# Block 0 of a fused attention, dense and expert kernel: its steps issued in another order

## The chip, the cores and the metric

The kernel runs on one core of one Trainium2 chip, as one launch. The metric is the device time in microseconds; lower is better. Five engines work side by side, each through its own instructions in program order, and wait for each other by semaphores: TensorE (PE in the rows: matrix products and transposes, results into PSUM), VectorE (DVE), ScalarE (ACT), GpSimd (POOL) and SyncE (SP, which issues most transfers).

## What is computed

Three layers follow each other on 3072 tokens (4 sequences of 768) of width 384:

```
for t in range(S):                      # per batch b and head h, D = 48
    cur = np.einsum('bhd,bhe->bhde', u[None] * kt, vt)
    y[:, :, t] = np.einsum('bhd,bhde->bhe', rt, state + cur)
    state = wt[:, :, :, None] * state + np.einsum('bhd,bhe->bhde', kt, vt)
x = y as (3072, 384)
h = x @ w_in                            # 384 -> 2048
x = (maximum(h, 0) + alpha * minimum(h, 0)) @ w_out
expert_idx = argmax of (x / |x|) @ (expert_emb / |expert_emb|).T / tau
out = gate * (maximum(x @ w1[e], 0) @ w2[e])     # the chosen one of 8 experts per token
```

## The kernel before, in words

The tokens are cut into 24 tiles of 128, and three tiles make a block: eight blocks. A tile first goes through chunked attention, then its block through the dense layer (2048 hidden features in 16 groups f of 128), then all tokens through the experts. The dense part is a software pipeline over a step counter T: step T = 16 j + f issues the first layer's product for group f of block j (`l1`, nine matmuls into `h_ps`, L409), and the second layer's for the group two steps back (`l2`, nine matmuls into `o_ps`, L433). Each value is carried as a high and a low part in a reduced float format, so that three products replace one. After `l1`, ScalarE scales `h_ps` by alpha into `m` (L413), VectorE takes the minimum of both (`m`, L414), ScalarE rounds it to the high part `gh` (L417), and VectorE subtracts for the low part `gl` (L423, function `l1_lo`).

During block 0 (T = 0 to 15, and a written-out list PLAN ahead of it, which includes `l1` of f = 0 and 1) three other kinds of work stand between these products:

- **Weight passes** `conv(q, ...)`: the weights come as 64-bit words in 16 staged groups c (even: w_in, odd: w_out; each serves two f). Pass 0 is ScalarE (L196), pass 1 two VectorE operations (L198, L199), pass 2 the high part on ScalarE (L210), pass 3 the low part on VectorE (L212). At step T, pass 0 handles c = T+4, pass 1 c = T+3, pass 2 c = T+3 and pass 3 c = T+2. When pass 3 of a group is issued, SyncE is told to load group c+4 into a free staging buffer (there are four).
- **Logit work** `wprime_a` and `wprime_b`: extra columns of w_out that give the router's logits directly. For each w_out group, `wprime_a` transposes the weights on TensorE (`wt_ps`, L232, two PSUM buffers) and ScalarE copies them out to `wt` (L234, L235); one step later `wprime_b` multiplies by the normalized expert rows `enT` (`wq_ps`, L243), and ScalarE copies (L247, L248).
- **Attention pieces** `ATT[q](n)` of the three tiles of block 1 (n = 3, 4, 5, whose pieces start at T = 0, 4, 8). Pieces 0 and 1 are the decay scans with what follows from them on VectorE (L261 to L267; L270, after which ScalarE reads the weights, L278). 6 and 7 prepare r and the diagonal (L288; `dg_ps`, L300; L304; L309). 2 and 3 transpose k (`kt_ps`, L323; `Kt`, L324) and make the scores (`a_ps`, L333; ScalarE `A`, L336; a GpSimd mask). 4 gives `y_ps` and the new state `u_ps` (L346 to L369). 5 transposes y into the next block's `xh`, `xl` (L383 to L385). For tile n they run at T = t0, t0+1, t0+2, t0+4, t0+6 and t0+7.

All small PSUM results (`kt_ps`, `a_ps`, `dg_ps`, `u_ps`, `y_ps`, `t_ps`, `wt_ps`, `wq_ps`, `ep`) take turns in one pool of three buffers, `ps_a`; `h_ps` has two buffers of its own. A product that takes its turn waits until the one three turns back has been read.

In PLAN, `aq.n` is attention piece q of tile n, `cq.c` a weight pass, `l1.f` a first-layer product, `p0.g` and `p1.g` the logit work, and `wN` N matmuls whose result nobody reads. `s` normalizes the eight expert rows and transposes them into `enT`. No scheduler intervenes: each engine's order is the order of issue.

Of the kernel before, what the change touches and what calls it, by code (L numbers as in the profile page):

```python
# [8 lines left out]
F32 = mybir.dt.float32  # L9
# [4 lines left out]
AF = mybir.ActivationFunctionType  # L14
# [12 lines left out]
KD = DM // 128  # L27
NE = 8
# [36 lines left out]
WPD = (2, 3)  # L65
# [4 lines left out]
OFF = 4  # L70
# [4 lines left out]
LAGS = [0, 1, 4, 4, 6, 7, 2]  # L75

LOADS = [(0, "w"), (0, "rk"), "id", "v", (0, "n"), "e", (1, "w"), (1, "rk"), (1, "n"), (2, "w"), (2, "rk"), (2, "n"), 0, 1, 2, 3, "u"]
PLAN = "a0.0 a1.0 a8.0 a2.0 w6 a6.0 a3.0 a7.0 w8 a0.1 a1.1 a6.1 a4.0 a3.1 a9.0 a2.1 c0.0 a7.1 a9.1 w8 a0.2 c0.1 c0.2 a1.2 a6.2 c1.0 a4.1 w8 a3.2 c1.1 a7.2 a5.0 a5.1 c2.0 w4 a4.2 p0.0 c3.0 a5.2 c2.1 c1.2 l1.0 c3.1 c2.2 l1.1 c0.3 c3.2 s p1.0 a8.1 a2.2 a9.2"

AT1 = [0, 4, 8]  # L80
AT = {2: [-1, 6], 3: [-4, 1, 7]}
# [12 lines left out]
def tile_main(ctx, tc, keep, x2d, tbl, att, w_in, w_out, alpha, u_row, u_col, emb, tau, w1, w2, cst, out):  # L94
    nc = tc.nc
    PE, DVE, ACT, POOL, SP = nc.tensor, nc.vector, nc.scalar, nc.gpsimd, nc.sync
# [12 lines left out]
    ps_a = ctx.enter_context(tc.tile_pool(name="ps_a", bufs=3, space=bass.MemoryType.PSUM))  # L109

    identr, idsx, wix, cnt = keep
    ident = identr.bitcast(F32)
# [6 lines left out]
    enT = cp.tile([128, KD, NE], F32, name="enT")  # L119
# [26 lines left out]
    en = att2[0:NE, LD:LD + DM]  # L146
# [10 lines left out]
    def load_att(n, part=None):  # L157
        if n not in ld_t:
            if n == 2:
                ld_t[n] = att2[:, 0:LD]  # L160
            else:
                ld_t[n] = ldp.tile([128, LD], F32, tag="ld", name="ld")
        m = LN + 2 * DM if n in ND else LN
        for s in {None: [slice(0, LN), slice(m, LD)] if n in ND else [slice(0, LD)], "w": [slice(LD - LW, LD)], "rk": [slice(0, LN)], "n": [slice(m, LD - LW)]}[part]:
            SP.dma_start(out=ld_t[n][:, s], in_=att[n][:, s])
# [10 lines left out]
    NG = 8  # L176
# [4 lines left out]
    def load_stage(kind, g):  # L181
        t = sgp.tile([128, GF * DM, 2], I32, tag="sg", name="stg")
        if kind == "in":
            for k in range(KD):
                SP.dma_start(out=t[:, k * GF * 128:(k + 1) * GF * 128, :], in_=w_in[:, k, 2 * g * GF * 128:2 * (g + 1) * GF * 128])
        else:
            SP.dma_start(out=t, in_=w_out[:, g * GF:(g + 1) * GF, :])
        stage[kind, g] = t

    def conv(q, kind, g):  # L190

        t = stage[kind, g]
        lw, hw = t[:, :, 0], t[:, :, 1]
        lf = lw.bitcast(F32)
        if q == 0:
            ACT.activation(out=lf, in_=lw.bitcast(U32), func=AF.Copy, scale=-0.936 * 2.0 ** -51, bias=-2.0)  # L196
        elif q == 1:
            DVE.scalar_tensor_tensor(out=lw, in0=hw, scalar=3, in1=lw, op0=ALU.logical_shift_left, op1=ALU.bitwise_or)  # L198
            DVE.scalar_tensor_tensor(out=lw, in0=hw, scalar=0x3FFFFFFF, in1=lw, op0=ALU.bitwise_or, op1=ALU.bitwise_and)  # L199
        else:  # L200
            h, g0 = divmod(g, NG // 2)
            if kind == "in":
                hi, lo = (w[:, :, g0 * GW:(g0 + 1) * GW] for w in win[h])
            else:
                if h == len(wout):
                    wout_half()
                hi, lo = (w[:, g0 * GF:(g0 + 1) * GF, 0:DM] for w in wout[h])
            f3 = lf.rearrange("p (a b) -> p a b", a=(KD if kind == "in" else GF))
            if q == 2:
                ACT.activation(out=hi, in_=f3, func=AF.Copy, scale=-1.0)  # L210
            else:
                DVE.scalar_tensor_tensor(out=lo, in0=f3, scalar=-1.0, in1=hi.bitcast(F32), op0=ALU.mult, op1=ALU.subtract)  # L212
                del stage[kind, g]
# [175 lines left out]
    def warm(n):  # L389

        for _ in range(n):
            t = ps_h.tile([128, 3, 128], F32, tag="h", name="idle")
            PE.matmul(out=t, lhsT=oneb, rhs=oneb.rearrange("p (o t) -> p o t", o=1).to_broadcast([128, 3, 128]), start=True, stop=True)
# [4 lines left out]
    g_t, m_t, o_t = {}, {}, {}  # L398
# [22 lines left out]
    def l1_lo(j, f):  # L421
        gh, gl = g_t[j, f]
        DVE.tensor_tensor(out=gl, in0=m_t.pop((j, f)), in1=gh.bitcast(F32), op=ALU.subtract)  # L423
# [376 lines left out]
    if True:  # L800
# [40 lines left out]
        for n in range(B0[NB - 1], NTILE):  # L841
            c, b = divmod(n, B)
# [5 lines left out]
        for n in range(NTILE):  # L848
            j = max(q for q in range(NB) if B0[q] <= n)
# [7 lines left out]
        def run(kind, *a):  # L857
            if (kind, *a) in ran:
                return
            if kind != "w":  # L860
                ran.add((kind, *a))
            if kind == "a":
                q, n = a
                ATT[q](n)
                m = n + 3 if n < 2 else n + 2
                if q in (4, 8, 9) and n != 2 and m < NTILE and (n > 2 or {("a", i, n) for i in (4, 8, 9)} <= ran):
                    load_att(m)
            elif kind == "c":
                q, c = a
                conv(q, ("in", "out")[c % 2], c // 2)  # L870
                if q == 3 and c + NSG < 2 * NG:
                    load_stage(("in", "out")[(c + NSG) % 2], (c + NSG) // 2)
            elif kind == "w":
                warm(*a)
            elif kind == "l":
                (l1, l2)[a[0] - 1](0, a[1])
            elif kind == "p":
                (wprime_a, wprime_b)[a[0]](a[1])
            else:
                DVE.tensor_scalar(out=en2, in0=en2, scalar1=1e-6, scalar2=None, op0=ALU.add)  # L880
                DVE.reciprocal(out=en2, in_=en2)
                ACT.activation(out=en, in_=en, func=AF.Copy, scale=en2)
                ep = ps_a.tile([128, KD, NE], F32, tag="a", name="ep")
                for k in range(KD):
                    PE.transpose(ep[:, k, :], en[:, k * 128:(k + 1) * 128], ident[0:NE, 0:NE])
                ACT.activation(out=enT, in_=ep, func=AF.Copy)

        def pieces(T, qs):
            for q, n in sched.get(T, []):
                if q in qs:  # L890
                    run("a", q, n)
                    if q == 6:
                        run("a", 7, n)

        def convs(T, late):
            for q, i in CONV[late]:
                c = T + OFF - i
                if 0 <= c < 2 * NG:
                    run("c", q, c)
# [43 lines left out]

        for t in PLAN.split():
            run(t[0], *(int(i) for i in t[1:].split(".") if i))
        for T in range(16 * NB + 2):
            j, f = divmod(T, 16)
            for i, d in enumerate(WPD):
                c = T + OFF - d
                if c % 2 and 0 <= c < 2 * NG:  # L950
                    run("p", i, c // 2)
            convs(T, 0)
            pieces(T, (2, 3, 4, 5))
            if 0 <= T and j < NB:
                run('l', 1, f) if j == 0 else l1(j, f)
            if T == 16 * (NB - 1):
                xg.extend(atp.tile([128, 2, ROW], F32, tag=t, name="xg") for t in ("st", "st", "at"))
                for t in xg:
                    POOL.memset(t, 0.0)
            if T >= 2:  # L960
                run('l', 2, T - 2) if T < 18 else l2((T - 2) // 16, (T - 2) % 16)
                if (T - 2) % 16 == 15:
                    o_evac((T - 2) // 16)
                    q = (T - 2) // 16
                    bg.append(chain(route(q), *((early_table(), early_loads()) if q == NB - 2 else (last_table(),) if q == NB - 1 else ())))
            if T >= 0:
                pieces(T, (0, 1, 6, 8))
                convs(T, 2)
                if (j, f) in m_t:
                    l1_lo(j, f)  # L970
                convs(T, 1)
            step(STEP7 if j >= NB - 1 else 1)
            if T == 32:
                zero = sgp.tile([128, DM], F32, tag="sg", name="zero")
                POOL.memset(zero, 0.0)
            if 32 <= T < 32 + NTILE:
                SP.dma_start(out=out[(T - 32) * CH:(T - 31) * CH, :], in_=zero)
            for fn, i, at in EARLY:
                if T - 16 * NB == at:
                    (split, x_T)[fn](0, i)  # L980
# [350 lines left out]
```

## Time and profile before

| | us |
|---|---|
| median of 3 runs (lowest, highest) | 824.95 (823.55, 826.72) |
| the profiled execution's own time | 825.29 |
| its span, first to last instruction | 823.5 |
| TensorE busy, weight loads busy | 791.7, 753.9 |
| VectorE, ScalarE, GpSimd busy | 584.3, 436.4, 297.3 |
| mean granted TensorE clock | 0.989 of full |

The profiled execution lies 0.34 us above the median of the runs. Granted clock 1.00 is 2.4 GHz and 0.50 is 1.2 GHz. The span begins with some 34 us of first loads and attention of block 0, then come block 0's dense steps up to about 123 us, then seven blocks, and the experts. A busy share here is an average over all of them; only the stretch from about 12 to 123 us is touched by the change.

### The profile page before, as it was taken

To read this page: it belongs to the slowest core of one execution; us is meant where nothing else is said; L and a number is where in the kernel's file an instruction comes from. 1 tells how busy PE (TensorE), PEld (TensorE's weight loads), DVE (VectorE), ACT (ScalarE), POOL (GpSimd) and SP (SyncE) were. 2 spreads that over 40 slices of the span, in tenths; PEclk is the share of its full clock that TensorE was granted. 3 is DMA by queue.
4 is the path that set the end of the run, shared out by engine and by line. 5 is a ranking of instruction groups with operands and counts; after the bars stand their busy time and mean duration, and the time that the engine had idled before them with its cause. 6 is when DMAs were issued, how large, how long until landed. Compare 5 with 4: busy or idle time off the path is not lost. (4 is left out here: it accounts for less than half of the span.)

```text
span 823.5 us, 16482 instructions
## 1 busy us (share of the span) xinstructions
PE 791.7 (96%) x6462; PEld 753.9 (92%) x6462; DVE 584.3 (71%) x1229; ACT 436.4 (53%) x861; POOL 297.3 (36%) x365
## 2 busy tenths in 40 slices
PE   8788999999999999999999999998899999999996
PEld 5588899998999999999999999896899999999996
DVE  7879857886686586686676674637987677768662
ACT  5676645444345435444444443326556776767662
POOL 2101112233224124124224212154466776767731
PEclk9979999999999999999999999999999999999998
DMA  9555410235324313113113101054756787687740
GB/s 325 186 163 168 180 69 2 75 118 135 121 84 146 127 33 102 69 58 98 69 69 97 68 2 30 30 215 150 189 204 208 274 289 241 223 275 224 265 165 33
DMA packets 31623, 114.86 MB, mean 139 GB/s; under 512 B 5756, under 2 KB 13148, under 8 KB 29232
## 3 DMA queue, kind: packets, MB, share of 16 engines
q0 software_dynamic: 13952, 59.86, 22.1%
q1 hardware_dynamic: 17584, 53.85, 19.6%
q8 instruction: 53, 0.87, 0.5%
q14 instruction: 34, 0.28, 0.2%
HBM read 99.36 MB, written 15.51 MB: 139 GB/s over the span
## 5 line engine op out<-in xcount | busy, mean ns | idle before, releaser
L413 ACT ACTIVATE m<-h_ps,al_sb 128x384 f32<-128x384 f32 x128 | 74.1, 579 | 125.2 <-PE h_ps L409 120.3
L414 DVE TENSOR_TENSOR m<-h_ps,m 128x384 f32<-128x384 f32 x128 | 71.0, 554 | 97.8 <-ACT m L413 97.0
L417 ACT ACTIVATE gh<-m 128x384 fp32r<-128x384 f32 x128 | 67.2, 525 | 122.6 <-DVE m L414 122.0
L423 DVE TENSOR_TENSOR gl<-m,gh 128x384 fp32r<-128x384 f32 x128 | 80.6, 630 | 35.0 <-ACT gh L417 34.3
L337 POOL TENSOR_SCALAR_AFFINE_SELECT A<-A 128x512 f32<-128x512 f32 x48 | 30.3, 654 | 186.8 <-ACT A L336 186.8
L686 POOL DMA_INDIRECT raw<-in_w,wix x64 | 67.4, 1053 | 51.3 <-DVE w0l L698 23.2
L728 PE MATMUL h_ps<-yh,w0h 128*128 128x256 f32 x264 | 77.1, 292 | 3.4 <-DVE g2l L733 2.7
L728 PE MATMUL h_ps<-yl,w0h 128*128 128x256 f32 x264 | 74.7, 283 | 0.9 <-DVE yl L719 0.9
L728 PE MATMUL h_ps<-yh,w0l 128*128 128x256 f32 x264 | 74.3, 281 | 0.0
L698 DVE TENSOR_TENSOR w1l<-raw,w1h 128x768 fp32r<-128x768 f32 x64 | 60.7, 954 | 18.5 <-ACT w1h L697 14.5
L409 PE MATMUL h_ps<-xh,win0h 128*128 128x384 f32 x192 | 69.3, 361 | 2.3 <-DVE m L414 1.5
L698 DVE TENSOR_TENSOR w0l<-raw,w0h 128x768 fp32r<-128x768 f32 x64 | 60.7, 958 | 12.2 <-ACT w0h L697 11.3
L409 PE MATMUL h_ps<-xh,win1h 128*128 128x384 f32 x192 | 68.3, 356 | 0.2 <-DVE m L414 0.2
L433 PE MATMUL o_ps<-wout1h,gh 128*128 128x392 f32 x192 | 65.3, 340 | 0.5 <-issue 0.4
L433 PE MATMUL o_ps<-wout0l,gh 128*128 128x392 f32 x192 | 65.7, 342 | 0.0
L433 PE MATMUL o_ps<-wout1h,gl 128*128 128x392 f32 x192 | 65.4, 341 | 0.2 <-issue 0.2
L433 PE MATMUL o_ps<-wout0h,gh 128*128 128x392 f32 x192 | 65.7, 342 | 0.0
L409 PE MATMUL h_ps<-xl,win0h 128*128 128x384 f32 x192 | 65.5, 341 | 0.2 <-DVE xl L385 0.2
L433 PE MATMUL o_ps<-wout0h,gl 128*128 128x392 f32 x192 | 65.5, 341 | 0.0
L433 PE MATMUL o_ps<-wout1l,gh 128*128 128x392 f32 x192 | 65.4, 340 | 0.0
L409 PE MATMUL h_ps<-xh,win0l 128*128 128x384 f32 x192 | 65.3, 340 | 0.0
L409 PE MATMUL h_ps<-xh,win1l 128*128 128x384 f32 x192 | 64.9, 338 | 0.0
(282 smaller groups left out, 2258.5 us busy)
## 6 DMA issues: line engine op xcount, KB each, us to landing
ld<-in_att SPq DMA_DIRECT2D x18, 1348.5 KB, 5.6
stg<-in_w_in SPq DMA_DIRECT2D x24, 256.0 KB, 4.9
stg<-in_w_out SPq DMA_DIRECT2D x8, 768.0 KB, 4.0
x2d<-rows SPq DMA_DIRECT2D x24, 194.0 KB, 6.9
out<-zero SPq DMA_DIRECT2D x24, 192.0 KB, 6.9
ld<-in_att SPq DMA_DIRECT2D x5, 512.0 KB, 3.8
ld<-in_att SPq DMA_DIRECT2D x3, 452.5 KB, 5.2
raw<-in_w,wix POOLq DMA_INDIRECT x64
```

Of the source, the lines that this page charges most:

```text
L337: POOL.affine_select(out=h, in_=h, pattern=[[0, HP], [1, CH]], compare_op=ALU.is_gt, fill=0.0, base=0, channel_multiplier=-1)
L409: PE.matmul(out=h, lhsT=w[:, k, :], rhs=x[:, k, :], start=(n == 0), stop=(n == 3 * KD - 1))
L413: ACT.activation(out=m, in_=h, func=AF.Copy, scale=al_sb[:, f:f + 1])
L414: DVE.tensor_tensor(out=m, in0=h, in1=m, op=ALU.min)
L417: ACT.activation(out=gh, in_=m, func=AF.Copy)
L423: DVE.tensor_tensor(out=gl, in0=m_t.pop((j, f)), in1=gh.bitcast(F32), op=ALU.subtract)
L433: PE.matmul(out=o_t[j][i], lhsT=g[:, s], rhs=w, start=(f == 0 and n == 0), stop=(f == KF - 1 and n == 2))
L686: POOL.indirect_dma_start(out=t, out_offset=None, in_=src, in_offset=idx(wix[:, h, COL[s]:COL[s] + 1]))
L698: DVE.tensor_tensor(out=lo, in0=a, in1=hi.bitcast(F32), op=ALU.subtract)
L728: PE.matmul(out=h, lhsT=w[:, k, :], rhs=x[:, k, :], start=(n == 0), stop=(n == 3 * KD - 1))
```

## The change

Only the order of issue in PLAN and in block 0's steps is changed.

```
-PLAN = "... a6.1 a4.0 a3.1 a9.0 a2.1 c0.0 ... c3.0 a5.2 c2.1 c1.2 l1.0 c3.1 c2.2 l1.1 c0.3 c3.2 s p1.0 a8.1 a2.2 a9.2"
+PLAN = "... a6.1 s a4.0 a3.1 a9.0 a2.1 e c0.0 ... c3.0 a5.2 c2.1 c1.2 l1.0 c3.1 c2.2 l1.1 p1.0 c0.3 c3.2 w4 a8.1 a2.2 a9.2"
...
+            elif kind == "e":
+                ep = ps_a.tile([128, KD, NE], F32, tag="a", name="ep")
+                for k in range(KD):
+                    PE.transpose(ep[:, k, :], en[:, k * 128:(k + 1) * 128], ident[0:NE, 0:NE])
+                ACT.activation(out=enT, in_=ep, func=AF.Copy)
             else:
                 DVE.tensor_scalar(out=en2, in0=en2, scalar1=1e-6, scalar2=None, op0=ALU.add)
                 DVE.reciprocal(out=en2, in_=en2)
                 ACT.activation(out=en, in_=en, func=AF.Copy, scale=en2)
-                ep = ps_a.tile([128, KD, NE], F32, tag="a", name="ep")
-                for k in range(KD):
-                    PE.transpose(ep[:, k, :], en[:, k * 128:(k + 1) * 128], ident[0:NE, 0:NE])
-                ACT.activation(out=enT, in_=ep, func=AF.Copy)
...
             j, f = divmod(T, 16)
-            for i, d in enumerate(WPD):
-                c = T + OFF - d
-                if c % 2 and 0 <= c < 2 * NG:
-                    run("p", i, c // 2)
+            pieces(T, (2, 3, 4, 5))
             convs(T, 0)
-            pieces(T, (2, 3, 4, 5))
             if 0 <= T and j < NB:
                 run('l', 1, f) if j == 0 else l1(j, f)
...
-            if T >= 0:
-                pieces(T, (0, 1, 6, 8))
-                convs(T, 2)
-                if (j, f) in m_t:
-                    l1_lo(j, f)
-                convs(T, 1)
+            for i, d in enumerate(WPD):
+                c = T + OFF - d
+                if c % 2 and 0 <= c < 2 * NG:
+                    run("p", i, c // 2)
+            convs(T, 2)
+            if j == 0 and (j, f) in m_t:
+                l1_lo(j, f)
+            pieces(T, (0, 1, 6, 8))
+            if j and (j, f) in m_t:
+                l1_lo(j, f)
+            convs(T, 1)
```

So the expert rows (`s`, and their transposes, now `e`) go into the first loads' time; in PLAN the first `wprime_b` directly follows `l1` of f = 1, and four idle matmuls (`w4`) stand ahead of tile 2's k transposes; in each step attention pieces 2 to 5 come ahead of weight passes 0 and 1, the logit work comes behind both layers' products, and pieces 0, 1, 6 and 8 come behind weight pass 3 and `l1_lo`.

On ScalarE, at steps 3 and 4, before the change (`gh` of step 3 is the second row; `A` holds tile 3's scores):

```order
L413 ACTIVATE m<-h_ps,al_sb 128x384
L417 ACTIVATE gh<-m 128x384
L210 ACTIVATE win0h<-stg 128x3x256
L247 ACTIVATE s_wp<-wq_ps 128x16
L248 ACTIVATE wout0h<-s_wp 128x2x8
L196 ACTIVATE stg<-stg 128x768
L324 ACTIVATE Kt<-kt_ps 128x512
L336 ACTIVATE A<-a_ps 128x512 x2
L413 ACTIVATE m<-h_ps,al_sb 128x384
```

And in the changed kernel:

```order
L413 ACTIVATE m<-h_ps,al_sb 128x384
L417 ACTIVATE gh<-m 128x384
L234 ACTIVATE wt<-wt_ps_815 128x512
L235 ACTIVATE wt<-wt_ps_816 128x256
L210 ACTIVATE win0h<-stg 128x3x256
L324 ACTIVATE Kt<-kt_ps 128x512
L336 ACTIVATE A<-a_ps 128x512 x2
L196 ACTIVATE stg<-stg 128x768
L413 ACTIVATE m<-h_ps,al_sb 128x384
```

The two copies out of `wt_ps` now stand directly behind `gh` of step 3, where the copy of `wq_ps` stood behind a weight pass; and the weight pass L196 has moved behind the scores. The same holds at steps 7 and 8, and 11 and 12.

On VectorE, at step 1 (the second scan of tile 3, L270), before:

```order
L198 SCALAR_TENSOR_TENSOR stg<-stg 128x768
L199 SCALAR_TENSOR_TENSOR stg<-stg 128x768
L270 SCALAR_TENSOR_TENSOR PS<-ld,anew 128x519
L212 SCALAR_TENSOR_TENSOR wout0l<-stg,wout0h 128x2x384
L423 TENSOR_TENSOR gl<-m,gh 128x384
L198 SCALAR_TENSOR_TENSOR stg<-stg 128x768
L199 SCALAR_TENSOR_TENSOR stg<-stg 128x768
L414 TENSOR_TENSOR m<-h_ps,m 128x384
```

And in the changed kernel:

```order
L198 SCALAR_TENSOR_TENSOR stg<-stg 128x768
L199 SCALAR_TENSOR_TENSOR stg<-stg 128x768
L212 SCALAR_TENSOR_TENSOR wout0l<-stg,wout0h 128x2x384
L423 TENSOR_TENSOR gl<-m,gh 128x384
L270 SCALAR_TENSOR_TENSOR PS<-ld,anew 128x519
L198 SCALAR_TENSOR_TENSOR stg<-stg 128x768
L199 SCALAR_TENSOR_TENSOR stg<-stg 128x768
L414 TENSOR_TENSOR m<-h_ps,m 128x384
```

The scan has moved two operations back. The same holds at step 5 for tile 4 and at step 9 for tile 5. The order of SyncE's transfers is the same in both kernels.

## Rows read from the trace of the kernel before

**Rows 1.** Busy time by stretch: us, then PE, PEld, DVE, ACT, POOL, granted clock, DMA.

```profile
34.00:51.00 17.00, 10.46 (x142) 9.41 (x142) 13.55 (x21) 13.01 (x28) 0.89 (x2) 0.60 0.59 188
...
60.00:83.00 23.00, 20.71 (x260) 19.24 (x259) 20.54 (x31) 16.14 (x34) 3.71 (x6) 1.00 0.54 179
...
106.00:123.00 17.00, 17.00 (x198) 16.51 (x196) 8.06 (x14) 7.83 (x16) 3.42 (x5) 1.00 0.24 84
```

**Rows 2.** Timeline of TensorE: start, duration, instruction, idle before it and releaser.

```profile
37.96 0.48 PE L885 MATMUL ep<-ident,att 8*128 8x8 f32 x3 [3.94 <-ACT att L882]
...
45.29 0.89 PE L243 MATMUL wq_ps<-enT,wt 128*32 128x8 f32 x48 [1.63 <-ACT wt L234]
...
46.59 0.52 PE L409 MATMUL h_ps<-xl,win0h 128*128 128x384 f32 x1
...
48.84 0.52 PE L409 MATMUL h_ps<-xh,win0l 128*128 128x384 f32 x1
...
56.35 0.59 PE L243 MATMUL wq_ps<-enT,wt 128*32 128x8 f32 x48
...
58.39 1.16 PE L333 MATMUL a_ps<-ld 64*128 64x128 f32 x14 [0.45 <-ACT s_wp L247]
59.47 0.44 PE L409 MATMUL h_ps<-xh,win0h 128*128 128x384 f32 x1
```

**Rows 3.** Timeline of VectorE.

```profile
15.37 0.56 DVE L369 TENSOR_TENSOR y<-y_ps,dv 128x384 f32<-128x384 f32 x1 [1.78 <-PE y_ps L367]
...
37.43 0.96 DVE L198 SCALAR_TENSOR_TENSOR stg<-stg 128x768 int32<-128x768 int32 x1 [0.27 <-ACT stg L196]
...
43.85 0.96 DVE L198 SCALAR_TENSOR_TENSOR stg<-stg 128x768 int32<-128x768 int32 x1 [1.12 <-ACT stg L196]
...
45.72 1.23 DVE L270 TENSOR_TENSOR_SCAN PS<-ld,anew 128x519 f32<-128x519 f32 x1
...
50.98 0.56 DVE L414 TENSOR_TENSOR m<-h_ps,m 128x384 f32<-128x384 f32 x1 [0.83 <-ACT m L413]
...
52.69 0.56 DVE L309 TENSOR_TENSOR dv<-ld,dg 128x384 f32<-128x384 f32 x1 [0.55 <-ACT dg L304]
...
56.36 0.55 DVE L414 TENSOR_TENSOR m<-h_ps,m 128x384 f32<-128x384 f32 x1
...
68.98 1.23 DVE L270 TENSOR_TENSOR_SCAN PS<-ld,anew 128x519 f32<-128x519 f32 x1
70.13 0.93 DVE L212 SCALAR_TENSOR_TENSOR wout0l<-stg,wout0h 128x768 fp32r<-128x768 f32 x1
...
71.45 0.95 DVE L198 SCALAR_TENSOR_TENSOR stg<-stg 128x768 int32<-128x768 int32 x1
```

**Rows 4.** Timeline of ScalarE.

```profile
39.62 0.18 ACT L247 ACTIVATE s_wp<-wq_ps 128x16 f32<-128x16 f32 x1 [0.95 <-PE wq_ps L243]
...
46.98 0.72 ACT L278 ACTIVATE ld<-ld,wmid 128x512 f32<-128x512 f32 x1 [0.68 <-DVE PS L270]
...
50.39 0.56 ACT L413 ACTIVATE m<-h_ps,al_sb 128x384 f32<-128x384 f32 x1
...
53.38 0.59 ACT L234 ACTIVATE wt<-wt_ps 128x512 f32<-128x512 f32 x1
...
56.95 0.52 ACT L417 ACTIVATE gh<-m 128x384 fp32r<-128x384 f32 x1 [1.44 <-DVE m L414]
...
70.25 0.72 ACT L278 ACTIVATE ld<-ld,wmid 128x512 f32<-128x512 f32 x1 [0.62 <-DMA stg<-in_w_in]
...
73.55 0.58 ACT L413 ACTIVATE m<-h_ps,al_sb 128x384 f32<-128x384 f32 x1
```

**Rows 5.** TensorE alone by stretch: us, busy, granted clock, DMA share, GB/s.

```profile
37.00:38.00 1.00, 0.04 (x1) 0.55 1.02 426
...
51.00:52.00 1.00, 1.00 (x10) 1.00 0.43 178
...
569.00:571.00 2.00, 0.15 (x2) 1.00 1.00 381
```

More of the change, by code (lines that the diff above doesn't have):

```diff
@@ L77 @@
 LOADS = [(0, "w"), (0, "rk"), "id", "v", (0, "n"), "e", (1, "w"), (1, "rk"), (1, "n"), (2, "w"), (2, "rk"), (2, "n"), 0, 1, 2, 3, "u"]
-PLAN = "a0.0 a1.0 a8.0 a2.0 w6 a6.0 a3.0 a7.0 w8 a0.1 a1.1 a6.1 a4.0 a3.1 a9.0 a2.1 c0.0 a7.1 a9.1 w8 a0.2 c0.1 c0.2 a1.2 a6.2 c1.0 a4.1 w8 a3.2 c1.1 a7.2 a5.0 a5.1 c2.0 w4 a4.2 p0.0 c3.0 a5.2 c2.1 c1.2 l1.0 c3.1 c2.2 l1.1 c0.3 c3.2 s p1.0 a8.1 a2.2 a9.2"
+PLAN = "a0.0 a1.0 a8.0 a2.0 w6 a6.0 a3.0 a7.0 w8 a0.1 a1.1 a6.1 s a4.0 a3.1 a9.0 a2.1 e c0.0 a7.1 a9.1 w8 a0.2 c0.1 c0.2 a1.2 a6.2 c1.0 a4.1 w8 a3.2 c1.1 a7.2 a5.0 a5.1 c2.0 w4 a4.2 p0.0 c3.0 a5.2 c2.1 c1.2 l1.0 c3.1 c2.2 l1.1 p1.0 c0.3 c3.2 w4 a8.1 a2.2 a9.2"
 AT1 = [0, 4, 8]
```

## The prediction, made before the changed kernel ran

> **What bounds the kernel now.** First the busy times by stretch, since the change touches only the time up to 123 us. From 34 to 51 us, where TensorE's longest waits lie, TensorE is busy 10.46 of 17.00 us at a mean clock of 0.60, while VectorE is busy 13.55 and ScalarE 13.01 [rows 1]. From 60 to 83, a stretch with one attention tile in it, VectorE (20.54 of 23.00) and TensorE (20.71) are close to each other; from 106 to 123 TensorE works all 17.00 us and VectorE less than half of them [rows 1].
>
> Then the timelines, for who waits last. TensorE stands 3.94 us before the expert rows' transposes `ep` and 1.63 us before the second `wq_ps` [rows 2]. Its clock falls while it stands: 0.55 in the slice from 37 to 38, and full again in the slice from 51, after it had worked without a gap since 45.29 [rows 2, 5]. That looks like some 5.6 us of waiting to be had, and more at the low clock. But what does the next step wait for? `m` of step 2 on VectorE starts at 50.98 and waited 0.83 us for ScalarE's `m` at 50.39, not for a product [rows 3, 4]. ScalarE is behind because it stood 0.68 us for the scan L270, up to 46.98 [rows 4]. And L270 started at 45.72 because VectorE had been working since 37.43, with a single wait, the 1.12 us before 43.85 [rows 3]. So in this stretch the path goes through the weight passes and the scan on VectorE and ScalarE; TensorE waits beside them. That is what the reader is to see: the largest idle time of the busiest engine is here not on the path.
>
> **The change, step by step.** Times are those of the profiled execution (825.29 us), which is 0.34 above the median of the runs; the sum is carried over to the median.
>
> (a) Expert rows early. Their two tiny VectorE operations fall into the 1.78 us for which VectorE waits before 15.37 [rows 3], and ScalarE waits for the same products. Without that cover they would cost under 1 us. The transposes `ep` are new in TensorE's row there and take one of the three `ps_a` turns, so that `dg_ps` of tile 1 waits for a copy. `ep` took 0.48 us at its old place, at a low clock [rows 2]. Between nothing and 0.48 I take +0.3, which TensorE hands on to the first `l1`.
>
> (b) The first `wprime_b` no longer waits, but its copies now stand ahead of weight pass 0 of group 3 on ScalarE. L247 takes 0.18 [rows 4]; with L248, about as long, I estimate 0.35. VectorE's row of passes therefore starts 0.65 later, at 38.08 in place of 37.43 [rows 3]. Its 1.12 us wait goes, because tile 2's `Kt` and state come sooner. L270 is now behind L212 and `gl`, which take 71.45 - 70.13 = 1.32 us [rows 3]. So L270 starts at 45.72 + 0.65 - 1.12 + 1.32 = 46.57 and ends at 47.80 in place of 46.95. From L278 to `m` ScalarE took 50.39 - 46.98 = 3.41 us [rows 4]; the copies L247 and L248 are no longer between, which leaves 3.06. `m` of step 2 on VectorE comes at 47.83 + 3.06 + 0.59 = 51.48: half a microsecond later than before.
>
> (c) From there to `m` of step 3 took 56.36 - 50.98 = 5.38 us, 0.55 of it a wait for `dg` [rows 3]. With L212 and `gl` ahead of its reader that wait goes: 51.48 + 4.83 = 56.31, level with before.
>
> (d) The new wait. Tile 3's scores `a_ps` take the turns of the two `wt_ps` of step 3, whose copies stand behind `gh`. After `m` ends at 56.86, `gh` takes 0.52, L234 0.59 [rows 4], and L235, with half of its columns, about 0.3: 58.3. Behind the waiting scores stands all of TensorE's row, and ScalarE's `m` of step 4. Before, TensorE waited until 58.39 for the copy of `wq_ps`, and `l1` of step 4 began 1.08 us later, at 59.47 [rows 2]. Now it begins at about 59.4: nothing gained. So the 5.6 us turn into a longer wait a few steps on, and (a) to (d) sum to -0.1.
>
> A page speaks for more. The Trainium skill (Perfetto Trace Analysis, Identifying the Most-Contended Engine) says that one improves a kernel by improving its most contended engine; over the whole span that is TensorE, and by this the 5.6 us would come off. For the stretch itself the rows name VectorE.
>
> (e) The clock. `l1` and `l2` of steps 2 and 3 no longer wait for the logit work and are done early, by about 49 us: weight pass 1 of group 3 ends near 40, and then come two steps of 18 matmuls each, at half of the low-clock spacing (48.84 - 46.59) / 7 = 0.32 us [rows 2], about 3 us a step, with small products between. Until 58.3 TensorE then has only one `wt_ps` and one `kt_ps` to do, so it stands about 8 of 9 us, in one piece for over 4. After 3.94 us the clock was low [rows 2, 5], so I expect 1.2 GHz when the scores start. `l1` of step 4 then loses 9 x 0.16 = 1.4 us and the scores up to 1.1. From below nothing, if the clock holds; from above 2.5. The rise before took more than 5 us of unbroken work [rows 2, 5], as long as both products take at 1.2 GHz, so nearer the upper end: +1.9.
>
> (f) Step 5 has the same shift as step 1: L270 of tile 4 starts 1.32 later. Its old end, 68.98 + 1.23 = 70.21 [rows 3], is what released L278 at 70.25 (the row names a transfer that ended about then), and `m` of step 6 followed at 73.55, 3.30 us later [rows 4]. Less 0.35 for L247 and L248, which are now behind `gh`: +1.0. At step 9 the same shift is hidden, since VectorE itself then adds state (tile 5 has no L352 on ScalarE) and is the later one.
>
> (g) The tail. From 106 us TensorE is the bound [rows 1]. The `wq_ps` of group 13, 0.59 us [rows 2], was issued ahead of `l1` of step 12 and now comes behind it: +0.6.
>
> The four idle matmuls fall into TensorE's wait for `Kt`, the later GpSimd copies into idle GpSimd time. SyncE's order is unchanged, and pass 3 now stands earlier in each step, so staging loads are issued no later. These cost nothing while VectorE is the later engine; otherwise the idle matmuls cost about 1 us.
>
> Sum: -0.1 + 1.9 + 1.0 + 0.6 = +3.4, so 828.7 on the profiled execution and 828.3 as a median.
>
> **Rivals.**
> *The clock holds* in (e): +1.5, so 826.4. For it: from 569 to 571 TensorE was busy 0.15 of 2.00 us and kept 1.00 [rows 5]; the small products in the gap might do the same. Against it: the last part of the gap is longer than 3.94.
> *TensorE's waits are the path*: 3.94 + 1.63 come off, less 0.3: -5.3, so 819.7. This is the faster side, and the page above goes with it. It decides itself at one point: `m` of step 2 on VectorE must come before about 49 us. For it: TensorE is the busiest engine over the span. Against it: VectorE's unbroken row from 43.85 to 50.98 - 0.83 = 50.15 [rows 3].
> *A second fall of the clock*: the wait of (d) returns, at about 2 us each, at the state product of step 6, the scores of step 8, `y_ps` of step 10 and the scores of step 12. If the clock falls in two of them, as at 37 us, each costs about as much as (e): +3.8 more, so 832.1. Against it the row at 569.
>
> **How the numbers follow.** Forecast 0.58 (own range 826 to 831), clock holds 0.16, TensorE is the path 0.14, second fall 0.12. A change of 0.5% is 4.1 us, about what a measurement can tell from none: bounds 820.8 and 829.1. Faster is most of the second rival, 0.10. Slower is the last rival and somewhat over a quarter of the forecast's own spread, 0.28. Same is 0.62. The range from 820.5 to 832.0 leaves out the lower half of one rival and the upper half of another, and a little of the spread.
>
> **What would show it.** Right: `m` of step 2 at 51 to 52 us although TensorE no longer waits for `ep`; `l1` of step 3 before 48; a wait of over 3 us before tile 3's scores, released by L234 or L235; clock 0.50 behind it; L278 of tile 4 a microsecond later after `m` of step 5 than before. Wrong: `m` of step 4 before 58 us, or scores that don't wait for L234. Block 1's first `l1` moves by the whole sum; what happens behind it should not differ. If I am wrong, most likely because ScalarE and VectorE have more slack around 40 us than I read, or because the clock does not fall.

## The result: slower by 0.77%

The changed kernel takes 832.26 us as a median of 5 runs (829.10 to 832.62), the kernel before 824.95 (823.55 to 826.72, here of 5 runs too): a ratio of 1.0077 with a 95% interval of 1.0052 to 1.0102 (the medians alone give 1.0089). Two stray executions of the kernel before, 958.83 and 4323.61 us beside e1 to e4 below, count in no ratio. The profiled execution is the shortest of the five, 829.1 us with a span of 827.2; the other four have spans of 830.3 to 830.8. So two things are to be explained: the 3.8 us by which the profiled execution is above that of before (829.1 - 825.29), and the 3 us more of the others.

Busy time by stretch in the changed kernel (columns as in [rows 1]):

```profile
34.00:51.00 17.00, 14.01 (x177) 12.39 (x176) 13.78 (x19) 11.64 (x23) 0.22 (x1) 0.90 0.63 199
51.00:60.00 9.00, 3.25 (x25) 2.82 (x23) 8.32 (x12) 6.10 (x14) 0.46 (x1) 0.70 0.39 108
60.00:83.00 23.00, 21.44 (x246) 20.27 (x244) 18.11 (x28) 14.01 (x29) 4.28 (x6) 0.89 0.50 174
106.00:123.00 17.00, 16.27 (x200) 15.28 (x198) 9.77 (x16) 8.54 (x18) 1.44 (x3) 1.00 0.13 39
```

TensorE's two waits around 40 us [rows 2] are gone, as the change wants, though one of 2.58 us ahead of tile 2's `u_ps` has come in place of 0.69 there. From 34 to 51 it works 14.01 us at a clock of 0.90, where it was 10.46 at 0.60 [rows 1]. But in the next 9 us it mostly stands: 3.25 us of work, at 0.70. TensorE's timeline has this `u_ps`, `l1` of step 3, the last products before the scores, the scores of tile 3, `l1` of step 4 and a later wait of the same kind:

```profile
39.53 0.56 PE L346 MATMUL u_ps<-att,Kt 128*48 128x48 f32 x16 [2.58 <-ACT Kt L324]
...
47.40 0.43 PE L409 MATMUL h_ps<-xh,win0h 128*128 128x384 f32 x1
...
52.85 0.50 PE L232 MATMUL wt_ps<-ident,stg 128*128 128x128 f32 x2 [1.55 <-ACT s_wp L247]
53.19 0.63 PE L323 MATMUL kt_ps<-ident,ld 128*128 128x128 f32 x4
58.02 2.35 PE L333 MATMUL a_ps<-ld 64*128 64x128 f32 x16 [4.20 <-ACT wt L234]
...
60.30 0.69 PE L409 MATMUL h_ps<-xh,win0h 128*128 128x384 f32 x1
...
71.51 0.77 PE L346 MATMUL u_ps<-ld,Kt 128*48 128x48 f32 x16 [1.56 <-ACT wt L234]
```

`l1` of step 3 starts at 47.40, early; then the scores of tile 3 wait 4.20 us for the copy L234, and the sixteen take 2.35, where fourteen of them took 1.16 in the kernel before [rows 2]. Four more waits for L234 follow up to 109 us, of 0.69 to 2.20. VectorE's timeline has the scans L270 of tiles 2 and 4 and `m` of steps 2 to 6:

```profile
46.74 1.23 DVE L270 TENSOR_TENSOR_SCAN PS<-ld,anew 128x519 f32<-128x519 f32 x1
...
51.61 0.56 DVE L414 TENSOR_TENSOR m<-h_ps,m 128x384 f32<-128x384 f32 x1 [1.79 <-ACT m L413]
...
56.37 0.55 DVE L414 TENSOR_TENSOR m<-h_ps,m 128x384 f32<-128x384 f32 x1
...
63.32 0.56 DVE L414 TENSOR_TENSOR m<-h_ps,m 128x384 f32<-128x384 f32 x1 [3.20 <-ACT m L413]
...
69.86 0.55 DVE L414 TENSOR_TENSOR m<-h_ps,m 128x384 f32<-128x384 f32 x1
...
71.66 1.23 DVE L270 TENSOR_TENSOR_SCAN PS<-ld,anew 128x519 f32<-128x519 f32 x1
...
76.69 0.56 DVE L414 TENSOR_TENSOR m<-h_ps,m 128x384 f32<-128x384 f32 x1 [1.48 <-ACT m L413]
```

ScalarE's has L278 behind these scans, the copies that free the scores' turns, and `m` of steps 4 to 6:

```profile
48.01 0.73 ACT L278 ACTIVATE ld<-ld,wmid 128x512 f32<-128x512 f32 x1 [3.73 <-DVE PS L270]
...
57.39 0.58 ACT L234 ACTIVATE wt<-wt_ps 128x512 f32<-128x512 f32 x1
57.87 0.37 ACT L235 ACTIVATE wt<-wt_ps 128x256 f32<-128x256 f32 x1
...
62.70 0.58 ACT L413 ACTIVATE m<-h_ps,al_sb 128x384 f32<-128x384 f32 x1 [0.62 <-PE h_ps L409]
...
66.81 0.57 ACT L413 ACTIVATE m<-h_ps,al_sb 128x384 f32<-128x384 f32 x1
...
72.93 0.72 ACT L278 ACTIVATE ld<-ld,wmid 128x512 f32<-128x512 f32 x1 [1.21 <-DVE PS L270]
...
76.07 0.58 ACT L413 ACTIVATE m<-h_ps,al_sb 128x384 f32<-128x384 f32 x1
```

In the kernel before, `m` of steps 4 and 6 on VectorE:

```profile
61.97 0.56 DVE L414 TENSOR_TENSOR m<-h_ps,m 128x384 f32<-128x384 f32 x1 [1.86 <-ACT m L413]
...
74.17 0.56 DVE L414 TENSOR_TENSOR m<-h_ps,m 128x384 f32<-128x384 f32 x1 [0.31 <-ACT m L413]
```

In the changed kernel, `m` of step 2 on VectorE starts at 51.61 (50.98 before [rows 3]), although TensorE no longer waits for `ep`; `m` of step 3 at 56.37, level with 56.36; `m` of step 4 at 63.32, which is 1.35 later than in the kernel before (61.97). The scan L270 of tile 4 starts at 71.66 (68.98 before [rows 3]), L278 behind it at 72.93, and `m` of step 6 comes at 76.69, 2.52 later than before (74.17).

The clock by stretch of TensorE alone (columns as in [rows 5]):

```profile
54.00:56.00 2.00, 0.00 (x0) 0.66 0.87 280
56.00:58.00 2.00, 0.00 (x0) 0.50 0.39 122
...
60.00:62.00 2.00, 2.00 (x10) 0.64 0.74 307
...
72.00:74.00 2.00, 2.00 (x14) 0.50 0.71 197
```

It goes to 0.50 (1.2 GHz) while TensorE stands before the scores and is still low at 60; it falls a second time behind the wait at 70.

### The profile page after: what moved, and what is told of

The parts are those of the page before. It is cut to its first block, busy times and chain, and to the rows that moved or that the text cites. A ratio compares the mean times of both kernels' runs of the same rounds, so it can differ in the third digit from the quotient of the medians.

```text
span 827.2 us, 16493 instructions
## 1 busy us (share of the span) xinstructions
PE 793.3 (96%) x6466; PEld 755.2 (91%) x6466; DVE 582.9 (70%) x1229; ACT 435.7 (53%) x861; POOL 293.3 (35%) x365
## 3 DMA queue, kind: packets, MB, share of 16 engines
HBM read 99.36 MB, written 15.51 MB: 139 GB/s over the span
```

## The experiments

The experiments ran in four groups, each on a chip of its own beside runs of the kernel before there, with medians of 824.31 (e1 to e4), 821.63 (e5 to e8), 821.91 (e9 to e11) and 825.75 us (e12); so ratios are compared, not times. An expectation given in microseconds is compared with the ratio times 824.31, the first group's median. No kernel leaves work out; idle matmuls add products that nothing reads. The change has four parts: early expert rows (A), attention pieces 2 to 5 ahead of pass 0 (B), logit work behind both layers (C), scans (pieces 0, 1, 6, 8) behind pass 2 and `gl` (D).

To see where in block 0 each profiled execution loses, this table gives the time from one step's `m` on VectorE to that of a later step, from the starts of these rows in each trace (us). Starts differ by what the prologue, the time ahead of `m` of step 0, did; the last column leaves that out.

| kernel | ratio to before (95%) | 1 to 2 | 2 to 3 | 3 to 4 | 5 to 6 | 6 to 7 | 9 to 10 | 10 to 11 | 13 to 15 | 0 to 16 |
|---|---|---|---|---|---|---|---|---|---|---|
| before | 1 | 15.48 | 5.38 | 5.61 | 5.65 | 5.35 | 6.02 | 5.35 | 9.50 | 92.22 |
| changed (ABCD) | 1.0077 (1.0052 to 1.0102) | 15.53 | 4.76 | 6.95 | 6.83 | 5.54 | 6.01 | 6.16 | 10.61 | 96.00 |
| e1, the same | 1.0083 (1.0059 to 1.0107) | 15.52 | 4.76 | 7.83 | 6.83 | 5.55 | 7.49 | 6.22 | 10.62 | 98.43 |
| e2, ABD | 1.0071 (1.0050 to 1.0093) | 15.85 | 4.75 | 7.13 | 7.15 | 5.67 | 6.29 | 5.49 | 9.50 | 96.27 |
| e3, ABC | 1.0107 (1.0079 to 1.0135) | 14.24 | 5.26 | 7.54 | 5.68 | 7.67 | 7.47 | 7.14 | 10.61 | 102.24 |
| e4, A | 1.0020 (1.0006 to 1.0034) | 14.59 | 4.89 | 5.63 | 5.69 | 5.35 | 6.03 | 5.34 | 9.50 | 90.90 |
| e5, AB | 1.0015 (1.0004 to 1.0026) | 14.56 | 4.88 | 5.60 | 5.84 | 5.50 | 6.37 | 5.47 | 9.49 | 91.61 |
| e6, AC | 1.0075 (1.0057 to 1.0093) | 14.29 | 5.26 | 7.10 | 5.36 | 6.54 | 7.51 | 7.16 | 10.62 | 97.45 |
| e7, AD | 1.0055 (1.0040 to 1.0069) | 15.89 | 4.74 | 7.93 | 7.00 | 5.31 | 6.28 | 5.37 | 9.50 | 95.99 |
| e8, ABCD, waits filled | 1.0045 (1.0029 to 1.0060) | 15.51 | 4.77 | 5.50 | 6.82 | 5.56 | 6.02 | 6.15 | 10.61 | 94.52 |
| e9, AC to step 9, filled | 1.0064 (1.0051 to 1.0076) | 14.25 | 5.26 | 5.74 | 5.34 | 6.53 | 10.56 | 6.12 | 9.51 | 97.10 |
| e10, A, small waits filled | 0.9991 (0.9982 to 1.0000) | 14.57 | 4.89 | 5.62 | 5.68 | 5.35 | 6.02 | 5.34 | 9.49 | 90.93 |
| e11, before, `ep` wait filled | 1.0004 (0.9991 to 1.0017) | 14.80 | 5.55 | 5.63 | 5.65 | 5.36 | 6.03 | 5.48 | 9.49 | 91.97 |
| e12, before, small waits filled | 1.0007 (0.9994 to 1.0020) | 15.11 | 4.89 | 5.80 | 5.69 | 5.35 | 6.01 | 5.35 | 9.50 | 91.60 |

Behind `m` of step 16 the profiled executions of a group take nearly the same time to the end of the span, 697.9 to 698.8 us in e1 to e4 and 693.8 to 695.1 in e5 to e11, so what sets them apart lies mostly ahead of it. The prologue has its part in that: `m` of step 0 starts at 32.86 to 33.09 in the three profiles without A and at 33.23 to 33.99 in nine of the eleven with it. In e5 and e10 it starts at 34.69 and 34.90, and there the clock fell behind `ep` and the small products around it, as in e10:

```profile
20.00:22.00 2.00, 2.00 (x7) 0.50 0.92 313
```

**e1, the changed kernel again.** No edit.

> The changed kernel once more, as the measure for the other runs and for the 3 us between its profiled execution (829.1 us) and its other runs (832.3). Theory (standing for the copies behind gh lowers TensorE's clock): median 831 to 833; if the profile falls on a longer execution, block 1 starts some 3 us later than 127.3 us, with one more stretch at clock 0.50 between 60 and 123 us. Rival (the 3 us are lost behind block 0, in the staged loads of later blocks): block 1 starts at about 127.3 and the difference appears behind it. A profile at about 829 leaves this open.

831.28 us (829.90 to 833.94). The profile fell on a longer execution, 831.97. Its TensorE rows by stretch:

```profile
54.00:56.00 2.00, 0.00 (x0) 0.50 0.91 312
...
72.00:74.00 2.00, 2.00 (x25) 1.00 0.58 129
...
98.00:100.00 2.00, 2.00 (x19) 0.50 1.00 364
```

The clock held at 72, where it had fallen in the first profile, and fell at 98, where it had held. From `m` of step 3 to step 4 this execution takes 0.88 more than the first, from step 9 to 10 it takes 1.48 more, and the two are nearly all of the 2.43 by which its block 0 is longer; the whole execution is longer by 2.87. `m` of step 16 comes 2.00 later, since the prologue is 0.43 shorter, and the rest lies behind it. So the theory holds for this execution in the main: most of the 3 us are falls of the clock in block 0. The other runs have no profile.

**e2, logit work back at the head of the step.**

```diff
+            for i, d in enumerate(WPD):
+                ...
+                    run("p", i, c // 2)
             pieces(T, (2, 3, 4, 5))
             convs(T, 0)
```

> The changed kernel with the logit work back at the head of each step. Theory: tile 3's scores and the later products no longer wait for L234 and L235 behind gh, TensorE does not stand there, its clock stays up, and the wq_ps of group 13 is again ahead of l1: terms (e) and (g), 1.9 + 0.6, come off, and a second fall of the clock with them (up to 3.8): 826 to 829 us, no wait over 1 us on L234 at tile 3's scores. Rival (the later scans L270 are the cost, and the clock is incidental): at most 1 us comes off, 831 or more.

830.30 us, only 1.0 below e1 and within its noise: between the two, nearer the rival. Term (g) does come off (13 to 15 takes 9.50), and no wait for L234 is left before the scores. But one for L247, a copy that also stands behind `gh`, has its place:

```profile
58.36 1.34 PE L333 MATMUL a_ps<-ld 64*128 64x128 f32 x14 [2.40 <-ACT s_wp L247]
```

and the clock falls there all the same:

```profile
60.00:62.00 2.00, 2.00 (x7) 0.50 0.64 267
```

The kernel before has this copy at the same place and starts the scores at 58.39, but after a wait of only 0.45 [rows 2]: its TensorE comes later to them. So the wait of (d) does not hang on the logit work alone; a TensorE that runs ahead stands there too.

**e3, scans back ahead of pass 2.**

```diff
+            pieces(T, (0, 1, 6, 8))
             convs(T, 2)
             if j == 0 and (j, f) in m_t:
                 l1_lo(j, f)
-            pieces(T, (0, 1, 6, 8))
```

> The changed kernel with the scans (pieces 0, 1, 6, 8) back ahead of weight pass 2 and gl; the logit work stays behind both layers. Theory: L270 starts 1.3 us earlier, which is worth term (f), 1.0, and some 0.5 at step 2: 830 to 831.5 us, and the wait of tile 3's scores for L234 stays at 3 us or more with clock 0.50 behind it. Rival (the later scans are the main cost): 3 us or more come off, 829 or less.

835.20 us: against both. The six runs lie in two groups, 830.69 and 831.40, and 835.20 to 835.99, and the profile fell on the longest. Term (f) does come off (5 to 6 takes 5.68), and step 2 is 1.3 earlier, but the profiled execution loses 2.3 us from step 6 to 7 and 1.3 to 1.9 in five other places, with the clock low in three more stretches:

```profile
83.00:90.00 7.00, 5.39 (x32) 0.76 0.52 170
...
97.00:106.00 9.00, 7.42 (x117) 0.81 0.75 256
106.00:123.00 17.00, 15.36 (x137) 0.90 0.06 25
```

TensorE stands 4.70 us before tile 3's scores and 1.61 before tile 4's (4.20 and 0.70 in the first profile of the changed kernel). Not all of this is the clock: from step 6 to 7 VectorE waits 2.05 us for `dg`, whose product now directly follows `wq_ps`; e6 has that at full clock. So an earlier scan does not help while the logit work stands behind both layers, and the parts don't add.

**e4, early expert rows alone.** The steps are as before; of the plan, a few tokens a line:

```diff
 a0.1 a1.1 a6.1
+s
 a4.0 a3.1 a9.0 a2.1
+e
...
 l1.1
+p1.0
 c0.3 c3.2
-s p1.0
+w4
 a8.1 a2.2 a9.2
```

> The kernel before with the expert rows early and nothing else moved in the steps (the plan of the start as in the change). Theory (VectorE's and ScalarE's row of weight passes and scans sets the time around 40 us, TensorE's 3.94 us wait for ep lies beside it): the wait goes, m of step 2 still comes at 50.5 to 51.5 us, 824.5 to 826 us. Rival (TensorE's waits are the path): some 4 to 5 us come off, 820 to 821.

826.23 us, a ratio of 1.0020. TensorE's 3.94 us wait is gone, and `m` of step 2 starts at 50.33, 0.17 below what the theory allowed; nothing of the rival's 5 us is seen. But a wait of 2.59 us ahead of `u_ps` has come, and the 1.62 us before the second `wq_ps` stays, so that of some 6.5 us of waiting up to 45 us only 2.3 came off; e11 is the cleaner test. The wait before tile 3's scores:

```profile
57.25 1.16 PE L333 MATMUL a_ps<-ld 64*128 64x128 f32 x14 [1.23 <-ACT s_wp L247]
```

Block 0 of the profiled execution is 1.3 us shorter than before, yet the runs are not faster; e10 comes back to that.

**e5, e6, e7: one further part each on top of e4.**

```diff
# e5
-            convs(T, 0)
             pieces(T, (2, 3, 4, 5))
+            convs(T, 0)
# e6
-            for i, d in enumerate(WPD):
-                ...
-                    run("p", i, c // 2)
             convs(T, 0)
...
             if T >= 2:
...
+            for i, d in enumerate(WPD):
+                ...
+                    run("p", i, c // 2)
             if T >= 0:
                 pieces(T, (0, 1, 6, 8))
# e7
-                pieces(T, (0, 1, 6, 8))
                 convs(T, 2)
                 ...
+            pieces(T, (0, 1, 6, 8))
```

> The kernel with early expert rows (826.23 us) and, besides, only the attention pieces 2 to 5 ahead of pass 0 in each step. Theory (the later scans make ScalarE's m later, TensorE stands longer for it, and its clock falls): this part does little, 825.5 to 828 us, m of step 4 within 0.5 of 60.85 us, clock 1.00 from 51 to 123 us. Rival (it is the piece order that the slow versions share): 829 or more, m of step 4 at 62.5 or later.

> The kernel with early expert rows and, besides, only the logit work behind both layers' products. Theory: tile 3's scores wait 3 us or more for L234 behind gh and the clock falls to 0.50 behind it, 828 to 833 us. Rival (the wait is beside the path and the clock holds): 825 to 827.5.

> The kernel with early expert rows and, besides, only the scans (pieces 0, 1, 6, 8) behind weight pass 2 and gl. Theory: m of step 2 comes some 1.3 us later than 50.33, tile 3's scores wait over 2 us where they waited 1.23, the clock falls at 60 us and again at one or two later waits: 829 to 831 us, as the run with the logit work at the head (830.3). Rival (the piece order is the cause there): 826 to 828.

823.12, 826.97 and 826.13 us beside 821.63. The order of the pieces (B) adds nothing to e4 (1.0015 against 1.0020), as its theory had it. On the first group's scale C (e6) comes to 830.5, inside its theory's range, and D (e7) to 828.8, just short of its theory's 829. So C and D each make a slow kernel alone, and the largest loss that they share is TensorE's wait before tile 3's scores. In e6, TensorE's row of that wait:

```profile
57.01 2.35 PE L333 MATMUL a_ps<-ld 64*128 64x128 f32 x16 [4.69 <-ACT wt L234]
```

and its busy time and clock in the stretch:

```profile
56.00:60.00 4.00, 2.99 (x18) 0.50 0.74 251
```

In e7 the row of the wait:

```profile
58.97 2.07 PE L333 MATMUL a_ps<-ld 64*128 64x128 f32 x14 [2.54 <-ACT s_wp L247]
```

and the stretch behind it:

```profile
60.00:64.00 4.00, 4.00 (x17) 0.50 0.42 166
```

With C the scores wait 4.69 for L234, with D 2.54 for L247, since `m` of step 3, on which `gh` ahead of that copy waits, starts at 56.94 (55.22 in e4); in e4 they wait 1.23 and the clock stays. `m` of step 4 then follows step 3's after 7.10 and 7.93 in place of 5.63. In e6 a second cost of C shows, apart from the clock: `dg_ps` stands directly behind `wq_ps` on TensorE, and VectorE waits for it at step 6:

```profile
76.34 0.66 DVE L309 TENSOR_TENSOR dv<-ld,dg 128x384 f32<-128x384 f32 x1 [0.82 <-ACT dg L304]
```

From step 6 to 7 e6 loses 1.19 and from step 10 to 11, where this wait is 1.54, it loses 1.81, both at a clock of 1.00.

**e8, the changed kernel with its waits filled.** 24 idle matmuls ahead of tile 3's scores, and 9, 6, 12 and 4 at four later waits.

```diff
+    def fill(n):
+        t = ps_h.tile([128, 3, 128], F32, tag="h", name="idle")
+        for _ in range(n):
+            PE.matmul(out=t, lhsT=oneb, rhs=oneb.rearrange("p (o t) -> p o t", o=1).to_broadcast([128, 3, 128]), start=True, stop=True)
...
+        if n in FILL:
+            fill(FILL[n])
         a = [ps_a.tile([128, HP, CH], F32, tag="a", name="a_ps") for _ in range(2)]
```

> The changed kernel with idle matmuls in TensorE's waits of block 0: 24 ahead of tile 3's scores, 9 ahead of its state product, 6 and 4 ahead of the scores of tiles 4 and 5, 12 ahead of the products with the state of tile 4. They compute nothing that is read; the waits for ScalarE stay as they are. Theory (the falls of the clock behind the waits cost most of what the change loses): clock 1.00 from 54 to 123 us, m of step 4 at 62 us or earlier, 3 to 4 us off: 827 to 829 us. Rival (the waits themselves and the later scans are the cost): clock 1.00 too, but at most 1 us off: 830.5 or more. If the idle matmuls delay the products behind them, m of step 3 or 4 comes later than 63.5.

825.00 us, 1.0045, or 828.0 on the first group's scale, as the theory had it: half of the loss is gone, 3.4 us above the kernel before where e1 was 7.0 above (the intervals of the two ratios just touch). The clock by stretch:

```profile
54.00:58.00 4.00, 3.71 (x25) 1.00 0.53 185
...
70.00:76.00 6.00, 6.00 (x94) 1.00 0.84 298
```

TensorE's timeline at the scores (L336 here; L235 is the copy L234):

```profile
53.30 4.06 PE L405 MATMUL idle<-oneb 128*128 128x384 bf16 x24
57.66 0.65 PE L336 MATMUL a_ps<-ld 64*128 64x128 f32 x4 [0.29 <-ACT wt L235]
```

ScalarE's, with that copy and the read behind the scan of tile 4 (L279 here):

```profile
57.03 0.58 ACT L235 ACTIVATE wt<-wt_ps 128x512 f32<-128x512 f32 x1
...
71.13 0.72 ACT L279 ACTIVATE ld<-ld,wmid 128x512 f32<-128x512 f32 x1 [1.20 <-DVE PS L271]
```

The copy that releases the scores starts at 57.03, 0.36 earlier than in the first profile, and that is what the prologues differ by (`m` of step 0 at 33.31 and 33.66); so ScalarE is as late as it was, and only the clock differs. From `m` of step 3 to step 4 it takes 5.50, a little less than in the kernel before: the wait for the copy, still there, costs nothing by itself. What stays is the same as without the filling: 5 to 6 at 6.82, 10 to 11 at 6.15, 13 to 15 at 10.61; with what 2 to 3 gives back, block 0 to step 16 is 2.30 longer than in the kernel before.

**e9, a version put together.**

```diff
+                if T >= 10 and c % 2 and 0 <= c < 2 * NG:   # head of the step
+                    run("p", i, c // 2)
             ...
+                if T < 10 and c % 2 and 0 <= c < 2 * NG:    # behind l2
+                    run("p", i, c // 2)
```

> A version put together from what the steps showed: early expert rows; the logit work behind both layers up to step 9 and at the head of the step from step 10; pieces and scans where the kernel before has them; idle matmuls in TensorE's waits as in the run that filled them. Theory (the later scans, the falls of the clock and the logit work in the tail are what the change costs, each apart): 1.0 to 2.5 us faster than the kernel before, m of step 6 at 73 us or earlier, m of step 16 at 123 to 124.5, clock 1.00 from 54 to 123 us. Rival (what is won in block 0 is given back behind it, as the run with the early rows alone suggests, whose m of step 16 came 1.1 us earlier and whose median was 1.9 later): the same or slower than the kernel before by up to 2 us, although m of step 16 comes a microsecond earlier.

826.78 us, 1.0064: neither. Up to step 9 it does what was expected (`m` of step 6 at 72.94), except that step 6 to 7 takes 6.53, with 0.84 us of waiting for `dg` as in e6. Then it loses 4.5 us in one step, because the seam was put at step 10 and split a pair, `wprime_a` behind the layers of step 9 and its `wprime_b` at the head of step 10. TensorE there:

```profile
93.17 0.89 PE L244 MATMUL wq_ps<-enT,wt 128*32 128x8 f32 x48 [2.61 <-ACT wt L235]
...
94.81 3.12 PE L405 MATMUL idle<-oneb 128*128 128x384 bf16 x12
```

and ScalarE's `m` of step 10 (L425 here):

```profile
101.47 0.58 ACT L425 ACTIVATE m<-h_ps,al_sb 128x384 f32<-128x384 f32 x1 [5.43 <-PE h_ps L421]
```

`wq_ps` now waits 2.61 for L235 behind `gh`, and the 12 idle matmuls behind it, no longer in a wait, hold TensorE for another 3.12 us at the low clock (0.50 from 94 to 96 us). Filler that comes late is a delay.

**e10, early expert rows with the small waits filled; e11 and e12, the kernel before with its waits filled.** e10 and e12 put 7, 5 and 5 idle matmuls ahead of the scores of tiles 3 to 5 and 5 ahead of the `t_ps` of tiles 3 and 4; e11 puts 22 ahead of `ep`.

```diff
# e10 and e12
+FILL = {3: 7, 4: 5, 5: 5}
...
+        if n in (3, 4):
+            fill(5)
         tp = ps_a.tile([128, KD, CH], F32, tag="a", name="t_ps")
# e11
+                fill(22)
                 ep = ps_a.tile([128, KD, NE], F32, tag="a", name="ep")
```

> Early expert rows alone, with 5 to 7 idle matmuls in TensorE's five waits between 55 and 106 us. Theory (the 1.9 us of the run without them are falls of the clock in executions other than the profiled one, which kept 1.00): 1 to 2 us less than that run, within 1 us of the kernel before. Rival (the loss lies behind block 0): 1.5 to 2.5 us above the kernel before, as without them.

> The kernel before with 22 idle matmuls in the 3.94 us wait ahead of ep, and nothing else. Theory (neither this wait nor the low clock behind it is on the path): clock well over 0.64 from 34 to 45 us, m of step 2 and the time unchanged within 1 us. Rival (the wait itself is beside the path, but the low clock behind it costs): m of step 2 a microsecond or more earlier, 1 to 2 us faster.

> The kernel before with the same 5 to 7 idle matmuls in TensorE's five small waits between 55 and 106 us as in the run with the early rows, as its control. Theory (in the kernel before, a fall of the clock at these waits costs nothing, since TensorE is ahead there: with 0.54 from 74 to 76 us m of step 7 still followed m of step 6 by 5.36): within 0.6 us of the kernel before, clock 1.00 from 56 to 123 us. Rival (its executions lose to these falls too): 1 us or more faster, and then the early rows gave nothing beside the idle matmuls.

821.64 us against 821.91 (e10), 821.23 against 821.91 (e11), 825.73 against 825.75 (e12). Filling makes e4's order 0.29% faster (from 1.0020 to 0.9991, intervals that don't overlap) and leaves the order of before where it was. So what e4 loses is lost at those waits; that it is the clock there, in executions other than the profiled one, is inferred (idle matmuls end no wait sooner) and was not seen, since e4's profile kept 1.00 from 50 to 106 us. e11 shows the reverse for the kernel before. With its 3.94 us wait filled, TensorE's stretch from 34 to 45 us is:

```profile
34.00:45.00 11.00, 7.05 (x142) 0.93 0.72 235
```

In the kernel before the same stretch is:

```profile
34.00:45.00 11.00, 4.75 (x78) 0.64 0.70 231
```

Step 1 to 2 gets 0.68 shorter by it, step 2 to 3 gives back 0.17, and the ratio is 1.0004: no gain that can be told from noise. And its profile happens to show a fall at 74 us that costs nothing:

```profile
74.00:76.00 2.00, 1.31 (x5) 0.54 1.00 401
76.00:78.00 2.00, 2.00 (x9) 0.60 0.58 196
```

`m` of step 7 follows step 6's after 5.36, as at full clock. A second fall, with 0.52 from 98 to 100 us, goes with 0.13 more from step 10 to 11. No version beats the kernel before: e10 is level with it.

## Why the prediction was right or wrong

The mechanism was right, the size too small, and the side not the likeliest one. 828.3 was forecast, in a range from 820.5 to 832.0; the ratio of 1.0077 makes 831.3 of the kernel before, and the median itself, 832.26, lies 0.26 above the top. By the prediction's own bound of 829.1 that is slower, which had 0.28, where "same" had 0.62. For the profiled execution the sum was nearly right, 828.7 forecast and 829.1 measured, but in part by luck: at `m` of step 4 the change had cost 1.35 where 1.8 was forecast, at `m` of step 16 it had cost 4.35 (129.66 against 125.31) where 3.4 was, and the time behind that was some 0.7 us shorter than in the kernel before (697.5 against 698.2). The 832.1 of the rival with a second fall is close to the median as a number; what the four executions without a profile lost was not seen. Point by point, by its own steps:

**What bounds the kernel.** Right in the main, and shown by e4 and e11: removing or filling TensorE's longest wait brings `m` of step 2 forward by less than a microsecond, and the whole kernel gets no faster. The Trainium skill (Perfetto Trace Analysis, Identifying the Most-Contended Engine) would improve the most contended engine first. Over the span that is TensorE, and the runs disagree for this stretch, where the 3.94 us wait came off without a gain; by the busy times of the stretch itself [rows 1] it is VectorE, and that agrees.

**(a)** +0.3 forecast. `m` of step 0 is 0.57 later in the first profile and 0.14 later in e1 (33.23): the size fits between. The two prologues in which the clock fell (e5, e10) were some 1.4 us later still; the term had no such case.

**(b), (c)** Right to 0.2: L270 at 46.74 (46.57 forecast), `m` of step 2 at 51.61 (51.48), of step 3 at 56.37 (56.31).

**(d)** The wait came where forecast and by the copies named: the copy L234 ends at 57.97, the scores start at 58.02 (58.3 forecast). TensorE stood 5.7 of the 9 us up to 58, not 8, and 4.20 of them in one piece. That the wait needs the logit work was too narrow: e7 has it without.

**(e)** Right in kind, shown by e8: with the clock held, 3 to 4 takes 5.50, without 6.95 and 7.83. So the fall costs 1.45 and 2.33; +1.9 was forecast. It varies with how long the low clock lasts: 0.64 from 60 to 62 us and 1.00 behind it in the first profile, 0.50 and then 0.68 from 62 to 64 in e1.

**(f)** +1.0 forecast, +1.17 measured with the clock held (6.82 against 5.65), and absent in every kernel without D (5.34 to 5.84).

**(g)** +0.6 forecast, +1.1 measured (13 to 15 takes 10.61 against 9.50 in every kernel with C in the tail). The term counted one `wq_ps`; two steps of the tail lengthen, 13 to 14 by 0.43 and 14 to 15 by 0.68. And a term was missing: from step 10 to 11 C costs 0.8, also with the clock held; in the first profile VectorE waits 0.16 us for `dg` and 0.37 for `xh` there, and TensorE's products for them now stand behind `wq_ps`. In e6, without D, the wait for `dg` is 0.82 at step 6 and 1.54 at step 10; this was not tried by itself.

**The step that failed** is, as far as the two profiles of the changed kernel show, the weighing of the second fall. The prediction put "Against it the row at 569" and gave it 0.12. That row shows a short stretch at 0.15 busy that kept its clock; it does not show that such stretches keep it. In the two profiled executions the first fall came both times, and the waits at 70 and 96 us each lowered the clock in one and not in the other. The rival's price of 1.9 for each of two falls was somewhat high: a fall costs only where the next `m` waits for TensorE. At 9 to 10 it cost 1.48; the fall at 72 us in the first profile cost nothing (5 to 6 takes 6.83 there, 6.82 with the clock held). The first fall in e1 lasted longer than in the first profile and cost 0.88 more. Chances should have been laid over how many of five waits lower the clock, not over one.

What stays open: the division of the 3 us in the executions without a profile, a fall in the prologue as in e5 and e10 among them, and where e4 loses in them.

## What to carry to other kernels

Ask of each wait of the busiest engine what the next consumer waits for last; if it is another engine's row, the wait is worth little (here under 1 of 3.94 us, and nothing in the whole), and removing it lets the engine run into the next wait earlier and stand longer. Copies that free a PSUM turn are part of TensorE's path: placed behind an activation that is itself late, they hold all of TensorE's row. And price a long stand twice, for the wait and for the low clock behind it, in each of the executions that may have it.

## What was not expected of the hardware

Nearly the same wait in the same program lowers the clock in one execution and not in the next: behind 1.56 us of waiting at 70 us the clock was 0.50 from 72 to 74, behind 1.42 us in e1 it was 1.00; behind 2.20 us before 96 it was 1.00 in the first and 0.50 in e1. Idle matmuls hold it: 24 of them in 4.06 us kept 1.00 where it had been 0.50. The Trainium skill (TensorE: Matmul & The Clock Gate, What's actually happening) says that "the default state is throttled, and activity releases the throttle"; e8 agrees, with a clock of 1.00 from 54 to 106 us. That a low clock costs nothing where TensorE is ahead is shown by e11, at 0.54 from 74 to 76 us. And the clock can fall where TensorE hardly stands: in e10 it was 0.84 from 18 to 20 us and 0.50 from 20 to 22, with 1.91 and 2.00 us of the two counted as busy, all of it small products up to 19.85 us.
